# One transfer and one scaling for the queries of two neighbouring pairs, in a kernel of block-sparse attention and a gated projection

## The chip, the cores and the metric

The kernel runs on one core of one Trainium2 chip. The metric is the device time of one execution in microseconds (us), lower is better. The kernel before was timed three times: 371.8, 375.03 and 377.35 us, median 375.03 us.

## The reference

Four batches of eight heads, 768 positions in 24 blocks of 32, head size 64. A query block sees its own block, both neighbours, the first and the last block and three blocks drawn for it; the first and the last query block see all 24. The result goes through a convolution gate and two 512x512 products.

```python
scores = scale * np.matmul(q, k.transpose(0, 1, 3, 2))        # scale = 1/8
scores = np.where(mask, scores, -1000000000.0)
attn = np.exp(scores - scores.max(-1)); attn = attn / attn.sum(-1)
x = np.matmul(attn, v)                                        # [4, 768, 512]
gate = 1.0 / (1.0 + np.exp(-gate_pre))                        # gate_pre: 5 taps over xp
return (gate * (x @ w_val) @ w_out).astype(np.float32)
```

## The kernel before

**Attention.** The unit of attention work is a pair of neighbouring query blocks, all eight heads: 11 pairs in a batch and one more, called global, for the first and last block, worked off in two units. That makes 13 units in a batch and 52 in all. For a unit TensorE (PE) multiplies queries and keys (tile `sc`, for the global pair `s`), VectorE (DVE) takes the row maxima (`mx`), ScalarE (ACT) the exponentials (`pe`, `rest`, `first`), PE transposes these (`pt`), ACT or DVE copies them to SBUF (`ptr`), PE multiplies with the values (`av`), DVE divides (`rs`, `x`), PE transposes back (`xp`) and a copy puts the result in `xT`. The loop over steps n (line 764) runs three units at once: the products of unit n, the transposes of unit n-1 and the values of unit n-2.

**What a unit loads.** `load_keys` (line 323) fetches the pair's queries with one transfer into `pr.qc`, one of five buffers of 128x256 numbers (128 partitions, 1 KB each), and in passing issues the transfers of a whole batch's keys (`k`, three of 512 KB) and values (`vn`, three of 520 KB) at the places that `K_AT` and `V_AT` name. The own and the drawn key blocks are gathered in `kg`, one of four buffers: POOL (GpSimd) copies the own blocks out of `k`; of the six drawn ones POOL and ACT copy three each in batch 0, POOL copies three and SyncE (SP) fetches three from memory in batch 1, and SP fetches all six in batches 2 and 3. The values of a pair come into `va` (three buffers, by SP) and, gathered by index, into `vb` (by POOL). There is one buffer of `vn`, so the first `vn` of a batch waits until the global pair of the batch before is through with it.

**Scaling.** `scale` (line 758) multiplies the pair's queries by 1/8 in place, on ACT in batches 0 and 1 and on DVE in batches 2 and 3 (`Q_ON`), two units ahead of the products (`SCALE_AHEAD`).

**The rest.** `decode_weights` turns the 64-bit weights (`wst`, loaded at the steps of `WEIGHTS_AT`) into two float parts each (`wv`, `wo`); `gates`, `split` and `project` are the gate (`th`), the splitting of `xT` (`xh`, `xl`) and the two products (`vp`, `op`, with `y`, `yh`, `yl` between), stored through `ot`. They fill the steps: `FILLS` says how many pieces of `project` go behind each half of a unit's transposes, `STEPS` how many pieces of decoding or gate. `project` can't start before all weights are decoded.

**Order.** Each engine runs its list in the order in which the program writes it (`InOrder`, line 83), and an instruction that waits holds up all behind it on its engine. SP issues all transfers of this text but the gathers by index; `pool.tile` buffers come free when the readers of the old content are done.

Every engine operation is recorded at line 89 in the profile, so the rows are told apart by their tiles.

Of the kernel before, what the change touches and what calls it, by code (L numbers as in the profile page):

```python
# [41 lines left out]
Q_ON = "AAVV"  # L42
OWN_ON = ("VP", "DP", "AD", "PP")
LOW_ON = "PVPPPPPP"
# [3 lines left out]
GATHER = "SUGGGGGGGUGSSSSGSUGSUSSGSSGGGSSGGGGGGGGGGGSGGGGGGGGGGUGG"  # L48

SP_VALUES = ((), (), (), ())  # L50
REGS = 4

FILLS = (
    "01111112111122232210210001"
    "11000100220213041124141102"
    "12011101111120112110020111"
    "11011121112101010101210101"
    "210341"
)
STEPS = (  # L60
    "10211005213213222312211222"
    "11302202121202021241340634"
    "23200312101440051090010133"
    "22234220022240100210033013"
    "101000"
)
# [4 lines left out]
def attention_moe(ctx, tc, qb, kb, v, ve, sampled, w_val, conv_w, w_out, ident_in, slot_in, out):  # L71
# [32 lines left out]

    sb = const.tile([128, NB, NR, 2], I32, name="sb")
    src = sampled.bitcast(I32)
# [3 lines left out]
    )  # L110
    slot = const.tile([128, 2 * NB + 1], F32, name="slot")
# [4 lines left out]
    ones = two.tile([128, 128], F32, tag="y", name="ones")  # L116
    dve.memset(ones, 1.0)
    opening = ps_moe.tile([128, 512], F32, tag="mo", name="opening")
    for n in range(OPENING):
        matmul(opening[:, 0:128], ones, ones, start=n == 0, stop=n == OPENING - 1)  # L120
    warm = const.tile([128, 1], F32, name="warm")
# [3 lines left out]
    dve.tensor_copy(sm, sb[0:1, :, :, 0].rearrange("p i r -> p (i r)"))  # L125
    sf = const.tile([128, NR, NB], F32, name="sf")
    dve.tensor_copy(sf, sb[:, :, :, 0].rearrange("p i r -> p r i"))
# [9 lines left out]
    dve.memset(valid[0:32, NB - 2 : NB - 1], 0.0)  # L137
    vm = const.tile([128, NR, NB], F32, name="vm")
    tmp = const.tile([128, NR, NB], F32, name="tmp")
    dve.tensor_scalar(out=vm, in0=sf, scalar1=0.0, scalar2=None, op0=ALU.not_equal)  # L140
# [67 lines left out]
    staged = []  # L208

    def load_weights():  # L210

        for n in range(2 * CH):
            st = const.tile([128, CH, TS], F32R, tag=("xh", "xl", "yh", "yl")[n % 4], name="wst")
            flat = st.bitcast(I32).rearrange("p c n -> p (c n)")[:, 0 : 2 * DM]
            c = n % CH
            sp.dma_start(flat, (w_val if n < CH else w_out).bitcast(I32)[c * 128 : (c + 1) * 128, :])
            staged.append((step[0], flat.rearrange("p (n w) -> p n w", w=2)))
            yield
# [58 lines left out]
    def load_batch(bt):  # L277
        b = bt.b
        bt.k = two.tile([128, NB, HP * BLK], F32, tag="k", name="k")
        for h in range(3):  # L280
            sp.dma_start(bt.k[:, 8 * h : 8 * h + 8, :], kb[:, b, 8 * h : 8 * h + 8, :])
            bt.loaded += 1
            yield
        assert b == 0 or batches[b - 1].valued == 2
        bt.vn = const.tile([128, S // 128, H * DV], F32, tag="vn", name="vn")
        for c in range(3):
            r0 = b * S + 256 * c
            sp.dma_start(
                bt.vn[:, 2 * c : 2 * c + 2, :], v[r0 : r0 + 256, :].rearrange("(c p) d -> p c d", p=128)
            )  # L290
            bt.loaded += 1
            yield
# [16 lines left out]
    def block_numbers(pr, eng):  # L309
# [195 lines left out]
    def values(un):  # L505
        pr = un.pr
        if un.e == 0:
            pr.av = ps_av.tile([128, 2, 2, DV], F32, tag="av", name="av")
        if pr.glob:
# [247 lines left out]

    def scale(pr):
        if Q_ON[pr.bt.b] == "A":
            act.activation(pr.qc, pr.qc, AF.Copy, scale=0.125)  # L760
        else:
            (dve if Q_ON[pr.bt.b] == "V" else pool).tensor_scalar(out=pr.qc, in0=pr.qc, scalar1=0.125, scalar2=None, op0=ALU.mult)

    for n in range(N + LAG_X):
# [25 lines left out]
        if k < 2 * CH and n >= WEIGHTS_AT[k] and (k < 4 or k - 4 in decoded):  # L790
            next(weights)

        if n < N:
            scores(units[n])
# [7 lines left out]
        if 0 <= n - LAG_V < N:  # L802
            values(units[n - LAG_V])
            if GATHER[n] == "W":
# [3 lines left out]
        if 0 <= n - LAG_T < N:  # L808
            for half, _ in enumerate(transposes(units[n - LAG_T])):
# [70 lines left out]
```

## Time and profile before

| what | us |
|---|---|
| median of the three runs | 375.03 |
| the profiled execution | 370.94 |
| its span, first to last instruction | 369.2 |
| PE busy in the span | 341.8 (93%) |
| DVE, ACT, POOL busy | 259.5, 245.9, 216.6 |
| PE's granted clock | 0.999 of full speed |

The span is the time from the first to the last instruction of the profiled execution; 1.74 us of its 370.94 us lie around it. An engine's busy time counts its instructions alone, without issuing transfers and without waits. DMA share is the mean busy share of the core's 16 DMA engines. In a row of waits the engine named after the arrow is the one whose work came last by the profile; "issue" means that the profile shows nothing that was waited for.

### The profile page before, as it was taken

The page shows a single profiled execution, that of the slowest core. Times are in us where ns is not written, and L with a number is a line of the kernel's source. Part 1 is how long each engine was busy: PE and PEld are TensorE (multiplying, and loading weights), DVE is VectorE, ACT ScalarE, POOL GpSimd, SP SyncE. Part 2 cuts the span into 40 slices and gives each one's busy share as a digit, 9 for nine tenths or more (in the row PEclk, how much of TensorE's full clock was granted, in tenths as well). Part 3 has the DMA queues.
Part 4 walks back from the last instruction along what each step waited for, and adds up shares of the span by engine and source line. Part 5 has one row for each costly group of instructions (what it writes and reads, how often), then busy time and mean ns, then how long its engine had stood idle before and what let it go on. Part 6 is the DMA issues. An engine that isn't in the chain of part 4 may idle for free.

```text
span 369.2 us, 15557 instructions
## 1 busy us (share of the span) xinstructions
PE 341.8 (93%) x6302; PEld 275.1 (75%) x6302; DVE 259.5 (70%) x561; ACT 245.9 (67%) x594; POOL 216.6 (59%) x318
## 2 busy tenths in 40 slices
PE   8777888996899999999999999998989999999995
PEld 8455556764676977787789778886878678989893
DVE  3556847879988689975978558984958737486920
ACT  2877697898698567867685667865555768545431
POOL 1785775788896476676652665565618444525440
PEclk9999999999999999999999999999999999999999
DMA  6999986999977686797686177988644454010202
GB/s 227 317 307 283 301 268 180 267 258 313 310 200 210 182 273 178 212 314 207 185 235 203 51 201 226 270 254 225 183 151 126 124 167 143 31 60 28 85 2 86
DMA packets 52440, 72.37 MB, mean 196 GB/s; under 512 B 6928, under 2 KB 34448, under 8 KB 52368
## 3 DMA queue, kind: packets, MB, share of 16 engines
q1 hardware_dynamic: 44896, 47.82, 42.2%
q0 software_dynamic: 7040, 23.43, 22.0%
q8 instruction: 50, 0.82, 0.9%
q14 instruction: 22, 0.18, 0.2%
q10 hardware_dynamic: 432, 0.11, 0.1%
HBM read 65.05 MB, written 6.29 MB: 193 GB/s over the span
## 4 chain that ended last, share of the span: by engine, by line
PE 66%; POOL 9%; DMA 7%; ACT 5%; issue 5%; DVE 4%; SPq 2%; POOLq 1%; ACTq 0%; DVEq 0%
PE op L89 16%; PE vp L89 15%; PE av L89 12%; PE pt L89 10%; PE sc L89 8%; POOL vb L89 4%; PE xp L89 2%; DMA k<-in_k 2%; PE s L89 2%; DMA va<-in_v 2%; ACT ptr L89 2%; POOL yl L89 2%; POOL kg L89 2%; ACT pe L89 1%; SPq L89 1%
## 5 line engine op out<-in xcount | busy, mean ns | idle before, releaser
L89 POOL DMA_INDIRECT vb<-in_v,idx x88 | 89.2, 1014 | 77.3 <-PE av L89 51.2
L89 DVE SCALAR_TENSOR_TENSOR th<-xT,cw,th 128x384 f32<-128x384 f32 x128 | 92.2, 732 | 8.8 <-ACT th L89 6.6
L89 ACT ACTIVATE pe<-sc,mx 128x256 f32<-128x256 f32 x176 | 69.2, 482 | 40.6 <-DVE mx L89 40.4
L89 DVE TENSOR_REDUCE mx<-sc 128x2 f32<-128x512 f32 x88 | 56.5, 683 | 35.0 <-PE sc L89 35.0
L89 ACT COPY ptr<-pt 128x512 f32<-128x512 f32 x105 | 60.7, 610 | 8.1 <-PE pt L89 6.2
L89 POOL COPY kg<-k 128x256 f32<-128x256 f32 (+1 forms) x154 | 52.7, 381 | 9.2 <-DMA k<-in_k 9.1
L89 PE MATMUL sc<-kg,qc 64*32 64x256 f32 x1408 | 53.2, 382 | 5.2 <-issue 2.5
L89 POOL TENSOR_TENSOR yl<-y,yh 128x384 fp32r<-128x384 f32 x32 | 33.0, 1034 | 39.4 <-ACT yh L89 39.3
L89 PE MATMUL op<-wo,yh 128*128 128x512 f32 x192 | 53.7, 401 | 0.0
L89 PE MATMUL pt<-ident,pe 128*128 128x128 f32 x352 | 50.7, 280 | 2.3 <-ACT rest L89 1.4
L89 PE MATMUL vp<-xh,wv 128*128 128x384 f32 x256 | 51.5, 343 | 1.2 <-ACT ot L89 1.2
L89 PEld LDWEIGHTS av<-va,ptr 128*32 128x32 f32 (+1 forms) x1056 | 30.5, 118 | 28.6 <-issue 10.8
L89 PE MATMUL av<-va,ptr 128*32 128x65 f32 (+1 forms) x1056 | 39.6, 226 | 9.4 <-DMA va<-in_v 3.7
L89 PEld LDWEIGHTS vp<-xh,wv 128*128 128x128 f32 x256 | 43.8, 188 | 1.6 <-ACT ot L89 1.4
L89 PEld LDWEIGHTS pt<-ident,pe 128*128 128x128 f32 x352 | 38.6, 140 | 8.5 <-ACT rest L89 1.7
L89 POOL TENSOR_TENSOR xl<-xT,xh 128x384 fp32r<-128x384 f32 x32 | 33.8, 1064 | 14.2 <-ACT xh L89 14.2
L89 PEld LDWEIGHTS sc<-kg,qc 64*32 64x32 f32 x1408 | 24.6, 106 | 21.0 <-issue 6.4
L89 PEld LDWEIGHTS op<-wo,yh 128*128 128x128 f32 x192 | 35.0, 188 | 6.9
L89 PE MATMUL av<-vb,ptr 128*32 128x65 f32 x1408 | 37.9, 222 | 1.3 <-issue 1.2
L89 PE MATMUL op<-wo,yl 128*128 128x512 f32 x96 | 31.6, 410 | 1.7 <-POOL yl L89 1.7
L89 PEld LDWEIGHTS av<-vb,ptr 128*32 128x32 f32 x1408 | 29.8, 110 | 3.3 <-issue 1.5
L89 DVE SCALAR_TENSOR_TENSOR y<-th,vp 128x384 f32<-128x384 f32 x32 | 17.6, 550 | 20.9 <-PE vp L89 16.0
(74 smaller groups left out, 455.8 us busy)
## 6 DMA issues: line engine op xcount, KB each, us to landing
kg<-in_k SPq DMA_DIRECT2D x165, 64.0 KB
vn<-in_v SPq DMA_DIRECT2D x12, 520.0 KB
qc<-in_q SPq DMA_DIRECT2D x48, 128.0 KB
k<-in_k SPq DMA_DIRECT2D x12, 512.0 KB
out<-ot SPq DMA_DIRECT2D x24, 256.0 KB
va<-in_v SPq DMA_DIRECT2D x44, 130.0 KB
wst<-in_w_val SPq DMA_DIRECT2D x4, 512.0 KB
wst<-in_w_out SPq DMA_DIRECT2D x4, 512.0 KB
```

Of the source, the lines that this page charges most:

```text
L89: made = getattr(self.eng, name)(*args, **kwargs)
```

## The change

Queries are loaded and scaled for two neighbouring pairs at once. The global pair and pair 0 keep a transfer of their own; pairs 1 and 2, 3 and 4, and so on to 9 and 10 share one of 128x512 numbers (256 KB), issued where the first of the two was issued, and one operation that scales all of it, where the first of the two was scaled. There are four buffers of two pairs in place of five of one.

```diff
+    four = ctx.enter_context(tc.tile_pool(name="four", bufs=QRING))      # QRING = 4
...
+    beside = {}
+
     def load_keys(pr):
         bt, b = pr.bt, pr.bt.b
-        pr.qc = five.tile([128, HP, 2, BLK], F32, tag="qc", name="qc")
-        sp.dma_start(pr.qc, qb[:, b, pr.p + 1])
+        if pr.p <= 0 or pr.p % 2:
+            pr.group = four.tile([128, 2, HP, 2, BLK], F32, tag="qc", name="qc")
+            many = 1 if pr.p <= 0 else 2
+            (act if Q_BY[b] == "A" else sp).dma_start(pr.group[:, 0:many], qb[:, b, pr.p + 1 : pr.p + 1 + many])
+            pr.whole = pr.group[:, 0:many]
+            pr.qc = pr.group[:, 0]
+            if pr.p > 0:
+                beside[b] = pr.group
+        else:
+            pr.whole = None
+            pr.qc = beside[b][:, 1]
...
     def scale(pr):
+        if pr.whole is None:
+            return
         if Q_ON[pr.bt.b] == "A":
-            act.activation(pr.qc, pr.qc, AF.Copy, scale=0.125)
+            act.activation(pr.whole, pr.whole, AF.Copy, scale=0.125)
```

The tables of the places of loads and of the pieces of work change with it:

```diff
-V_AT = ((2, 7, 8), (0, 1, 6), (2, 2, 6), (4, 6, 7))
-K_AT = ((9, 10, 11), (7, 8, 11), (2, 10, 11), (2, 5, 8))
+V_AT = ((1, 3, 7), (0, 0, 5), (2, 2, 3), (3, 6, 7))
+K_AT = ((8, 10, 10), (7, 8, 10), (0, 8, 8), (5, 5, 11))
-WEIGHTS_AT = (1, 3, 6, 7, 8, 10, 12, 15)
+WEIGHTS_AT = (1, 3, 6, 7, 7, 10, 11, 15)
-OWN_ON = ("VP", "DP", "AD", "PP")
+OWN_ON = ("DP", "DP", "AV", "PP")
 FILLS = (
-    "01111112111122232210210001"
+    "11011111011221220322102300"
...
 STEPS = (
-    "10211005213213222312211222"
+    "10121002253203322312210222"
...
```

Smaller edits: the small tiles of the index computation (`sb`, `slot`, `sf`, `vm`, `tmp`) become parts of one of the two `th` buffers, under the name `early`; the 31 opening matmuls write the bank of `av` instead of a bank of `ps_moe`; new tables `BULK_BY` and `Q_BY` (all on SP) and `KEEP` (all zero) stand for choices that are not taken.

What moves on the engines is shown at three places. The first is SP in batch 1, where it loads the queries of the global pair and pair 4; `kg` is a fetched key block, `va` is a pair's values, `qc` queries, `vn` a third of a batch's values, and the load of a register from `sm` opens the next unit's fetch of key blocks. Before:

```order
L89 DMA kg_159<-in_k 128x128
L89 DMA va_163<-in_ve 64x520
L89 DMA va_163<-in_v 64x520
L89 DMA qc<-in_q 128x256 x2
L316 TENSOR_LOAD sm
```

and now:

```order
L94 DMA kg_158<-in_k 128x128
L94 DMA va_162<-in_ve 64x520
L94 DMA va_162<-in_v 64x520
L94 DMA qc<-in_q 128x256
L94 DMA vn<-in_v 128x2x520
L337 TENSOR_LOAD sm
```

The batch's third `vn` now stands here; before it stood one unit later, behind the next unit's three `kg` transfers, its two `va` and one more `qc`.

The second place is ACT in batch 0, the units of pairs 4 and 5; `wv` is the high part of a decoded piece of weights. Before:

```order
L89 COPY ptr<-pt 128x512 x2
L89 CAST wv_164<-words 128x512
L89 COPY xT<-xp 128x4x64
L89 ACTIVATE qc<-qc 128x256
L89 ACTIVATE pe<-sc,mx 128x256 x4
L89 COPY ptr<-pt 128x512 x2
L89 COPY xT<-xp 128x4x64
L89 ACTIVATE pe<-sc,mx 128x256 x4
L89 COPY ptr<-pt 128x512
L89 CAST wv_164<-words 128x512
L89 COPY xT<-xp 128x4x64
L89 ACTIVATE qc<-qc 128x256
```

and now:

```order
L94 COPY ptr<-pt 128x512 x2
L94 COPY xT<-xp 128x4x64
L94 ACTIVATE qc<-qc 128x256
L94 ACTIVATE pe<-sc,mx 128x256 x4
L94 COPY ptr<-pt 128x512 x2
L94 CAST wv_163<-words 128x512
L94 COPY xT<-xp 128x4x64
L94 ACTIVATE pe<-sc,mx 128x256 x4
L94 COPY ptr<-pt 128x512
L94 CAST wv_163<-words 128x512
L94 COPY xT<-xp 128x4x64
```

One cast of weights moved one unit later, and the last scaling (of pair 6, the neighbour of pair 5) is gone.

The third place is DVE in batch 3, behind the global pair. Before:

```order
L89 TENSOR_SCALAR qc<-qc 128x256
L89 TENSOR_REDUCE mx<-sc 128x2 x2
L89 SCALAR_TENSOR_TENSOR th<-xT,cw,th 128x384 x4
L89 SCALAR_TENSOR_TENSOR y<-th,vp 128x384 x2
L89 TENSOR_SCALAR qc<-qc 128x256
L89 TENSOR_REDUCE mx<-sc 128x2 x2
```

and now:

```order
L94 TENSOR_REDUCE mx<-sc 128x2 x2
L94 SCALAR_TENSOR_TENSOR th<-xT,cw,th 128x384 x4
L94 SCALAR_TENSOR_TENSOR y<-th,vp 128x384 x2
L94 TENSOR_SCALAR qc<-qc 128x512
L94 TENSOR_REDUCE mx<-sc 128x2 x2
```

The scaling of pair 6 is gone and that of pair 7 is twice as wide, at its old place. POOL's list is the same before and now, and PE's differs in the bank of the opening matmuls and at three places where transposes change places with pieces of `vp` or `op`.

## Rows read from the trace of the kernel before

**Rows 1.** Busy time by stage: us, PE, PEld, DVE, ACT, POOL, clock, DMA share, GB/s.

```profile
0.00:57.00 57.00, 46.54 (x979) 35.02 (x979) 32.74 (x99) 39.21 (x110) 36.41 (x77) 1.00 0.88 277
57.00:80.00 23.00, 20.85 (x467) 15.28 (x474) 19.20 (x46) 19.93 (x56) 15.22 (x29) 1.00 0.87 248
80.00:100.00 20.00, 14.73 (x385) 10.70 (x376) 17.42 (x36) 15.49 (x38) 18.40 (x28) 1.00 0.99 307
100.00:122.00 22.00, 20.93 (x558) 16.06 (x557) 18.46 (x39) 20.13 (x51) 16.18 (x33) 1.00 0.72 197
122.00:240.00 118.00, 118.00 (x2174) 96.91 (x2175) 90.92 (x195) 82.25 (x194) 70.99 (x87) 1.00 0.72 212
240.00:300.00 60.00, 56.30 (x1140) 45.28 (x1139) 43.83 (x88) 36.28 (x83) 32.77 (x42) 1.00 0.60 175
```

**Rows 2.** Waits of PE, 0 to 122 us: total us, times, longest.

```profile
PE av L89 <- DMA va<-in_v: 3.7, 2, 2.3
PE av L89 <- ACT ptr L89: 2.7, 5, 1.0
PE sc L89 <- issue: 2.5, 4, 1.4
...
PE pt L89 <- ACT rest L89: 1.6, 3, 1.1
...
PE av L89 <- ACT wo L89: 0.9, 1, 0.9
...
PE sc L89 <- ACT pe L89: 0.8, 1, 0.8
PE av L89 <- ACT xT L89: 0.6, 1, 0.6
```

**Rows 3.** Groups of instructions: count, busy us, mean ns, idle before.

```profile
L89 POOL COPY kg<-k 128x256 f32<-128x256 f32 x88 | 36.9, 445 | 6.9 <-DMA k<-in_k 6.8
...
L89 DVE TENSOR_SCALAR qc<-qc 128x256 f32<-128x256 f32 x24 | 13.2, 551 | 0.0
L89 ACT ACTIVATE first<-s,mx 128x512 f32<-128x512 f32 x16 | 10.9, 681 | 0.2 <-PE pt L89 0.2
L89 ACT ACTIVATE qc<-qc 128x256 f32<-128x256 f32 x24 | 10.8, 456 | 2.7 <-DMA qc<-in_q 2.7
...
L89 ACT CAST wo<-words 128x512 fp32r<-128x512 f32 x4 | 2.6, 644 | 0.2 <-DVE words L89 0.2
```

**Rows 4.** SP's transfers and a product of PE in order of time: start us, us.

```profile
56.91 0.38 SPq L89 DMA_DIRECT2D vn<-in_v  x1
...
70.99 1.09 PE L89 MATMUL sc<-kg,qc 64*32 64x256 f32 x32
...
82.03 0.42 SPq L89 DMA_DIRECT2D vn<-in_v  x1
...
85.95 0.59 SPq L89 DMA_DIRECT2D va<-in_v  x1
```

**Rows 5.** Transfers on the chain that ended last: start us, us to landing.

```profile
71.62 4.38 DMA qc<-in_q
...
91.35 7.02 DMA va<-in_v
```

**Rows 6.** The tile qc: duration ns least, median, most, first and last start.

```profile
L89 DVE TENSOR_SCALAR qc<-qc x24: 279/288/4191, 133.7 to 295.5; 128x256 f32<-128x256 f32 x24
```

**Rows 7.** Engines in order of time, 280 to 289 us.

```profile
280.61 4.19 DVE L89 TENSOR_SCALAR qc<-qc 128x256 f32<-128x256 f32 x1
...
281.03 1.00 POOL L89 TENSOR_TENSOR xl<-xT,xh 128x384 fp32r<-128x384 f32 x1
...
283.65 0.99 POOL L89 TENSOR_TENSOR yl<-y,yh 128x384 fp32r<-128x384 f32 x1
...
288.83 0.34 PE L89 MATMUL av<-va,ptr 128*32 128x65 f32 x8 [0.83 <-ACT ptr L89]
```

**Rows 8.** ACT in order of time: a scaling in batch 1.

```profile
77.58 0.46 ACT L89 ACTIVATE qc<-qc 128x256 f32<-128x256 f32 x1
```

More of the change, by code (lines that the diff above doesn't have):

```diff
@@ L48 @@
 GATHER = "SUGGGGGGGUGSSSSGSUGSUSSGSSGGGSSGGGGGGGGGGGSGGGGGGGGGGUGG"
+BULK_BY = "SSSSSSSSSSSSSSSSSSSSSSSSSSSSSSSS"
+Q_BY = "SSSS"
+KEEP = "000000000000000000000000000000000000000000000000"
 SP_VALUES = ((), (), (), ())
@@ L53 @@
 FILLS = (
-    "01111112111122232210210001"
-    "11000100220213041124141102"
-    "12011101111120112110020111"
+    "11011111011221220322102300"
+    "10012110101421303120052002"
+    "12011101111120112110021011"
     "11011121112101010101210101"
-    "210341"
+    "214301"
 )
 STEPS = (
-    "10211005213213222312211222"
[L62 to L65, printed above, removed]
+    "10121002253203322312210222"
+    "11402202121202021214340634"
+    "32120032104140051900010222"
+    "23214330202240200013023013"
+    "000111"
 )
@@ L102, in attention_moe, with part @@
     matmul, transpose = pe.matmul, pe.transpose
-    sb = const.tile([128, NB, NR, 2], I32, name="sb")
+    early = two.tile([128, CH, TS], F32, tag="th", name="early").rearrange("p c n -> p (c n)")
+    def part(first, n, *dims):
+        names = "abc"[: len(dims)]
+        sizes = dict(zip(names, dims))
+        return early[:, first : first + n].rearrange(f"p ({' '.join(names)}) -> p {' '.join(names)}", **sizes)
+    sb = part(0, 2 * NB * NR, NB, NR, 2).bitcast(I32)
     src = sampled.bitcast(I32)
@@ L110, in attention_moe @@
     )
-    slot = const.tile([128, 2 * NB + 1], F32, name="slot")
+    slot = early[:, 160 : 160 + 2 * NB + 1]
     act.dma_start(slot, slot_in)
@@ L114, in attention_moe, with turn_over @@
     act.dma_start(ident, ident_in)
-    ones = two.tile([128, 128], F32, tag="y", name="ones")
+    ones = const.tile([128, 128], F32, name="ones")
     dve.memset(ones, 1.0)
-    opening = ps_moe.tile([128, 512], F32, tag="mo", name="opening")
-    for n in range(OPENING):
-        matmul(opening[:, 0:128], ones, ones, start=n == 0, stop=n == OPENING - 1)
+    bank_of_values = [ps_av.tile([128, 512], F32, tag="av", name="av")]
+    def turn_over(times):
+        for n in range(times):
+            matmul(bank_of_values[0][:, 384:512], ones, ones, start=n == 0, stop=n == times - 1)
+    turn_over(OPENING)
     warm = const.tile([128, 1], F32, name="warm")
@@ L125, in attention_moe @@
     dve.tensor_copy(sm, sb[0:1, :, :, 0].rearrange("p i r -> p (i r)"))
-    sf = const.tile([128, NR, NB], F32, name="sf")
+    sf = part(256, NR * NB, NR, NB)
     dve.tensor_copy(sf, sb[:, :, :, 0].rearrange("p i r -> p r i"))
@@ L137, in attention_moe @@
     dve.memset(valid[0:32, NB - 2 : NB - 1], 0.0)
-    vm = const.tile([128, NR, NB], F32, name="vm")
-    tmp = const.tile([128, NR, NB], F32, name="tmp")
+    vm = part(384, NR * NB, NR, NB)
+    tmp = part(512, NR * NB, NR, NB)
     dve.tensor_scalar(out=vm, in0=sf, scalar1=0.0, scalar2=None, op0=ALU.not_equal)
@@ L208, in attention_moe, with queue @@
     staged = []
+    def queue(n):
+        return act if BULK_BY[n] == "A" else sp
     def load_weights():
@@ L215, in load_weights @@
             c = n % CH
-            sp.dma_start(flat, (w_val if n < CH else w_out).bitcast(I32)[c * 128 : (c + 1) * 128, :])
+            queue(24 + n).dma_start(flat, (w_val if n < CH else w_out).bitcast(I32)[c * 128 : (c + 1) * 128, :])
             staged.append((step[0], flat.rearrange("p (n w) -> p n w", w=2)))
@@ L280, in load_batch @@
         for h in range(3):
-            sp.dma_start(bt.k[:, 8 * h : 8 * h + 8, :], kb[:, b, 8 * h : 8 * h + 8, :])
+            queue(3 * b + h).dma_start(bt.k[:, 8 * h : 8 * h + 8, :], kb[:, b, 8 * h : 8 * h + 8, :])
             bt.loaded += 1
@@ L287, in load_batch @@
             r0 = b * S + 256 * c
-            sp.dma_start(
+            queue(12 + 3 * b + c).dma_start(
                 bt.vn[:, 2 * c : 2 * c + 2, :], v[r0 : r0 + 256, :].rearrange("(c p) d -> p c d", p=128)
@@ L507, in values @@
         if un.e == 0:
-            pr.av = ps_av.tile([128, 2, 2, DV], F32, tag="av", name="av")
+            bank_of_values[0] = ps_av.tile([128, 512], F32, tag="av", name="av")
+            pr.av = bank_of_values[0][:, 0 : 4 * DV].rearrange("p (a h d) -> p a h d", a=2, h=2)
         if pr.glob:
@@ L758, in scale @@
     def scale(pr):
+        if pr.whole is None:
+            return
         if Q_ON[pr.bt.b] == "A":
-            act.activation(pr.qc, pr.qc, AF.Copy, scale=0.125)
+            act.activation(pr.whole, pr.whole, AF.Copy, scale=0.125)
         else:
-            (dve if Q_ON[pr.bt.b] == "V" else pool).tensor_scalar(out=pr.qc, in0=pr.qc, scalar1=0.125, scalar2=None, op0=ALU.mult)
+            (dve if Q_ON[pr.bt.b] == "V" else pool).tensor_scalar(
+                out=pr.whole, in0=pr.whole, scalar1=0.125, scalar2=None, op0=ALU.mult
+            )
     for n in range(N + LAG_X):
@@ L791, in attention_moe, with keep @@
             next(weights)
+        def keep(place):
+            turn_over(int((KEEP + "0000")[min(4 * n, len(KEEP)) + place]))
         if n < N:
+            keep(0)
             scores(units[n])
@@ L802, in attention_moe @@
         if 0 <= n - LAG_V < N:
+            keep(1)
             values(units[n - LAG_V])
@@ L808, in attention_moe @@
         if 0 <= n - LAG_T < N:
-            for half, _ in enumerate(transposes(units[n - LAG_T])):
+            turned = transposes(units[n - LAG_T])
+            for half in range(len(units[n - LAG_T].P)):
+                keep(2 + min(half, 1))
+                next(turned)
                 at_half = 2 * n + min(half, 1)
```

1 line of the change is left out of this document (added).

## Prediction

> **What bounds the kernel now.** I read the stage table first [rows 1], because the share of the whole span says little here: PE is busy 93%, yet the idle rest isn't spread evenly. From 122 to 240 us PE has no idle time at all. Its idle time is 10.46 us before 57 us (57.00 - 46.54), 2.15 us from 57 to 80, 5.27 us from 80 to 100, 1.07 us from 100 to 122, and 3.70 us from 240 to 300. So the change can gain in two places only: in batches 0 and 1, which have no projection to fill with, at most 18.95 us, part of it the start; and between 240 and 300 us, at most 3.70 us. In the saturated stretch a saving on another engine is hidden by PE's own work, and PE's work is the same before and after.
>
> The waits of PE before 122 us say what ended these gaps [rows 2]. Two waits for the transfer of `va` make 3.7 us. Those that end on ACT (`ptr`, `rest`, `wo`, `pe`, `xT`) make 2.7 + 1.6 + 0.9 + 0.8 + 0.6 = 6.6 us, and the products `sc` that wait for something that isn't named 2.5 us; these stand where ACT is late with freeing a score bank, so I count 9.1 us to ACT. In the same stages the DMA engines are 0.88, 0.87 and 0.99 busy [rows 1]. ACT and the transfers are what the change touches.
>
> **Part A: scaling on ACT, batches 0 and 1.** Removed are 24 operations of 128x256 at a mean of 456 ns, 10.9 us [rows 3]. Added are 4 of 128x256 (global pair and pair 0, twice), 1.8 us, and 10 of 128x512. The trace has no such scaling of 128x512, but casts of that size on ACT from SBUF to SBUF at 644 ns and exponentials from PSUM at 681 ns [rows 3]; the cast is nearer in source and destination: 6.4 us. Bounds: twice the narrow one, 912 ns, and the narrow one itself, 456 ns. So ACT has 10.9 - 8.2 = 2.7 us less to do. Not all of it reaches PE: a saving counts only in units in which PE waits for ACT. The five rows of ACT waits together with the unnamed ones have 15 waits in 26 units [rows 2], but some units have two; I take half of the units, 1.3 us. The other end is a loss: a wide scaling stands 0.19 us longer (644 - 456) before its unit's exponentials than the narrow one, and if just the ten units with a wide one are those on the path, PE loses 1.9 us. Range of the part: 1.9 us lost to 2.7 gained; taken: 1.3 gained.
>
> **Part B: the transfers.** 48 transfers become 28, 20 of them of 256 KB; the bytes stay the same. SP takes 0.38 to 0.59 us to issue a transfer [rows 4], so it issues some 20 x 0.45 = 9 us less over the kernel, half of that in batches 0 and 1. Where SP waits, this saves nothing: at 56.91 us it gets past the first `vn` of batch 1, which has to wait for the buffer [rows 4], and `V_AT` leaves that `vn` at the same place; all transfers ahead of it are the same ones in both kernels. Behind it order matters, for PE's two waits for `va` are due to transfers issued around 85.95 and 91.35 us [rows 4, 5], the second of which took 7.02 us to land while the DMA engines were 0.99 busy. The third `vn` stood just ahead, at 82.03 us, and now goes out one unit earlier, into a stage with 0.13 of 23 us free [rows 1], 3.0 us. Its 520 KB take 1.7 us at the stage's 307 GB/s; against that, the second half of a wide query transfer comes a unit earlier, 128 KB, 0.43 us. Taken: 1.7 - 0.4 = 1.3 us of the 3.7. Bounds: all 3.7 us gained; or nothing gained and 0.4 lost, if the free share doesn't lie where the `vn` now falls. The second `vn` now goes ahead of the first three `kg` of batch 1, which it delays by its 1.7 us; the products that need them start at 70.99 us [rows 4], 14 us behind that `vn`, which hides it.
>
> The Trainium skill (DMA: Bandwidth & Descriptors, section Bandwidth, Measured) says to batch transfers to 1 MiB or more for three quarters of the peak rate; its section on the anatomy of one DMA fits about 2 us of fixed cost to each, there for transfers that GpSimd issues. By that, as an estimate, 20 fewer transfers would be worth 40 us if they ran one behind the other. In the stage that matters the engines are 0.99 busy with several transfers at a time, so the fixed part lies beside other transfers; the sum goes without it, and the mechanism has its rival below.
>
> **Part C: scaling on DVE, batches 2 and 3.** Again 24 become 14, 10 of them wide. DVE spends 13.2 us on the 24, 551 ns each [rows 3], but the median is 288 ns and one took 4191 ns [rows 6]. That one stands beside a row of POOL instructions without a gap, from 281.03 to 284.64 us, and ends 0.16 us after them [rows 7]: DVE was held up, the maxima behind it were late, and PE waited 0.83 us for `ptr` soon after [rows 7]. Nothing says that this place is mended: POOL's list is unchanged, and the scaling that stood there stands there still, twice as wide. All others lie where PE is saturated or has no such wait. Taken: 0; bounds 1.2 us either way, the 0.83 and the like wait before it.
>
> The Trainium skill (SBUF — State Buffer, section Who interferes with whom) says that a DVE `tensor_scalar` can run in a mode in which it and a GpSimd instruction exclude each other, whoever comes first holding the port for the whole instruction. The row agrees in kind, but 4.19 us is the length of several POOL instructions, not of one. By the rule fewer scalings mean fewer such meetings, and the sum would gain up to the 1.2 us; by the row the meeting at 280.61 us stays.
>
> **Part D: the rest.** `OWN_ON[b]` in `copy_keys` reads the `b` of the function around it, which is 3 once the loops over batches are through; so all pairs use "PP" before and after, which the 88 copies of 128x256 on POOL (two for each of 44 pairs) confirm [rows 3]. The edit does nothing. Nor do `BULK_BY`, `Q_BY` and `KEEP`. `early` holds a `th` buffer that isn't needed until batch 0 is nearly through; the opening matmuls run on PE ahead of any `av`, so that bank costs no wait. `FILLS` moves three pieces on PE by a few matmuls, 0. `STEPS`, `WEIGHTS_AT` and `K_AT` move decoding by a unit and keys to earlier places; I see no wait that one of them ends or makes, and take 0. For their bounds I take one late cast of weights per batch, 0.9 us as in [rows 2], twice: 1.8 us either way.
>
> **Sum.** 1.3 + 1.3 + 0 + 0 = 2.6 us. The profiled execution, 370.94 us, would come to 368.3 us. It lies 4.1 us under the median of its own kernel; for a median I keep that distance: 375.03 - 2.6 = 372.4 us.
>
> **Rivals.**
> Nothing gained (375.0 us). ACT's saving falls into its own idle time and the `vn` only exchanges one wait for another. For it: ACT works 94.8 of the first 122 us (the sum of its busy time over four stages of [rows 1]), so it has 27 us of slack somewhere. Against: PE's waits for it are spread over many units.
>
> The cost per transfer is what holds batches 0 and 1 (366.5 us). Then fewer transfers free SP and the queue, and the whole of A and B comes: 2.7 + 3.7 us, with C's 1.2 and half of D's bound, 0.9: 8.5 us, that is 366.5. For it: the queries issued at 71.62 us took 4.38 us to land [rows 5], ten times what their bytes take at 307 GB/s. Against: 0.99 DMA share at 307 GB/s speaks for bytes, and those don't change. The rule on batching of the Trainium skill (DMA: Bandwidth & Descriptors, section Bandwidth) would show itself here in this way.
>
> The pair's transfer comes late (379.5 us, slower). A pair's queries are scaled on ACT one unit after their transfer is issued, and ACT runs in order. The transfer issued at 71.62 us landed after 4.38 us, at 76.0 [rows 5]; ACT scaled at 77.58 [rows 8], 5.96 us after the issue. A wide one lands 0.43 us later, still in time; but one that takes as long as the `va`, 7.02 + 0.43 us, makes ACT stand for 1.5 us, with the exponentials of a unit behind it. Three wide transfers of batch 1 fall into the busy stages: 4.5 us, 379.5 us; if all ten of batches 0 and 1 come late, 390. It decides from 5.96 us of landing on. Against: before, ACT waited for queries 2.7 us in all, at the start alone [rows 3].
>
> **How the numbers follow.** Forecast 0.52, nothing gained 0.21, cost per transfer 0.17, late transfer 0.10. A measurement of this kernel can tell about 2%, 7.5 us: faster is below 367.5, slower above 382.5. Most of the third case (0.13) and a tail of the forecast (0.02) lie below, 0.15; the worse part of the last (0.06) and 0.01 of table moves above, 0.07; 0.78 remain. The forecast's own range is 369.5 to 375. The range given runs from the third case, less the rest of D's bound (365.6), to the late transfer at three pairs (379.5).
>
> **What would show it.** Right: 14 scalings on ACT of 8 to 8.5 us in all; PE's waits for `va` before 100 us down from 3.7 to about 2.4; PE without idle time from 122 us, shifted earlier by some 2.5 us; DVE's long scaling near 280 us still there. Wrong: waits of ACT for `qc` after the start (late transfer); a DMA share in the first 57 us well under 0.88 with PE's waits gone (cost per transfer); PE's idle time before 122 us still near 19 us (nothing gained). If DVE's long scaling is gone and the time from 240 us on is shorter, part C was read wrongly; if a late piece of weights puts the first `vp` off, part D was.

## The result and the profile after

The changed kernel takes 375.42 us (median of 22 runs, 371.45 to 382.05), the kernel before 372.88 us (22 runs, 369.75 to 378.47): a ratio of 1.0062, 95% interval 1.0034 to 1.0089, so 0.6% slower where 0.7% faster was forecast. The ratios here and below leave disturbed runs out. The profiled execution of the changed kernel took 377.68 us and lies above its median, the one of before (370.94) below its own; the two profiles are 6.7 us apart, the medians 2.5. What follows shows where one long execution of the changed kernel loses time against one short execution of the kernel before; what it is worth, the experiments say.

The stage table of the changed kernel, with the columns of [rows 1]:

```profile
0.00:57.00 57.00, 47.18 (x979) 35.94 (x979) 33.59 (x102) 40.17 (x109) 35.54 (x76) 0.97 0.85 277
57.00:80.00 23.00, 21.86 (x502) 16.45 (x503) 20.53 (x46) 20.38 (x55) 18.62 (x32) 1.00 0.95 285
80.00:100.00 20.00, 14.99 (x339) 10.76 (x338) 14.31 (x27) 12.45 (x29) 17.53 (x27) 0.91 0.97 288
100.00:122.00 22.00, 18.57 (x430) 13.86 (x430) 16.06 (x35) 16.07 (x38) 12.84 (x23) 0.84 0.48 139
122.00:240.00 118.00, 114.93 (x2136) 94.13 (x2132) 87.33 (x186) 81.36 (x191) 70.93 (x93) 1.00 0.69 202
240.00:300.00 60.00, 57.44 (x1098) 46.73 (x1104) 47.06 (x87) 39.04 (x89) 34.06 (x43) 1.00 0.64 187
```

PE's waits up to 122 us, as in [rows 2]:

```profile
PE av L94 <- DMA vb<-in_v,idx: 4.8, 3, 2.3
PE pt L94 <- ACT rest L94: 3.9, 3, 2.0
PE sc L94 <- DVE th L94: 2.1, 1, 2.1
PE av L94 <- ACT ptr L94: 1.7, 4, 1.0
PE av L94 <- ACT qc L94: 1.5, 1, 1.5
...
PE s L94 <- DVE rs L94: 1.2, 1, 1.2
```

The waits for `va`, 3.7 us in [rows 2], are gone. In their place stand waits for the gathers `vb` (4.8), for `rest` (3.9 instead of 1.6) and for DVE (2.1 + 1.2). And the granted clock, 1.00 in every row of [rows 1], is 0.84 from 100 to 122 us. How much each counts in these two profiles is read at one point that both kernels pass with the same products behind them, the first `vp`. PE's row from the start to it, before and after:

```profile
0.00:121.72 121.72, 102.76 (x2374) 1.00 0.87 262
```

```profile
0.00:127.44 127.44, 108.04 (x2378) 0.95 0.81 249
```

The first `vp` comes 5.72 us later. PE's idle time up to it is 127.44 - 108.04 = 19.40 us, before 121.72 - 102.76 = 18.96: 0.44 us more. Its busy time for the same products is 5.28 us longer, and the clock is 0.95 in place of 1.00. So nearly all of the difference between these two profiles up to here stands in PE's busy time, not in its waits. The rest, 1.0 us, comes later: from 122 to 240 us PE is idle for 3.07 us where it had no idle time, and gets 1.14 us back from 240 to 300 and 0.87 behind that.

Two things limit this reading, as the same row shows of two kernels that lose nothing, e11 and e8 (the experiments describe them):

```profile
0.00:122.95 122.95, 106.31 (x2375) 0.99 0.84 259
```

```profile
0.00:125.46 125.46, 110.16 (x2374) 0.99 0.84 254
```

First, busy time is more than the clock. At 0.99 it is 3.55 and 7.40 us above that of the kernel before; time between the products of one group counts as busy too (the 192 products `s` up to 122 us are 6.7 us busy before and 10.2 in e8, at 381 and 382 ns each). Second, one profile isn't the kernel: the first `vp` comes at 125.46 us in e8, in a set where the kernel before was slower too, but also at 126.51 in e1, the same kernel in a set where it was not. So the 5.72 us are not the loss of the change.

Where the clock falls is seen on PE in order of time (changed kernel, waits in brackets):

```profile
37.36 0.30 PE L94 MATMUL av<-vb,ptr 128*32 128x65 f32 x2
39.98 0.72 PE L94 MATMUL av<-vb,ptr 128*32 128x65 f32 x30 [2.32 <-DMA vb<-in_v,idx]
40.63 1.97 PE L94 MATMUL pt<-ident,pe 128*128 128x128 f32 x8
...
76.19 1.09 PE L94 MATMUL pt<-ident,pe 128*128 128x128 f32 x8
...
82.02 1.09 PE L94 MATMUL av<-vb,ptr 128*32 128x65 f32 x30 [1.51 <-DMA vb<-in_v,idx]
83.04 1.94 PE L94 MATMUL pt<-ident,pe 128*128 128x128 f32 x8
...
89.86 2.25 PE L94 MATMUL s<-k,qc 64*32 64x256 f32 x48 [1.15 <-DVE rs L94]
...
94.92 1.09 PE L94 MATMUL pt<-ident,pe 128*128 128x128 f32 x8 [1.60 <-ACT rest L94]
...
101.37 1.52 PE L94 MATMUL pt<-ident,first 128*128 128x128 f32 x8 [2.01 <-ACT rest L94]
...
115.30 2.04 PE L94 MATMUL sc<-kg,qc 64*32 64x256 f32 x30 [2.05 <-DVE th L94]
...
120.44 1.09 PE L94 MATMUL sc<-kg,qc 64*32 64x256 f32 x32
```

Eight transposes take 1.09 us at 76.19 and 1.97 at 40.63, right behind a wait of 2.32 us; the scores, 1.09 us at 120.44, take 2.04 behind a wait of 2.05. PE's windows around these places (PE busy, granted clock, DMA share, GB/s) give a clock of 0.66, 0.53 and 0.57, a mix of stretches at 2.4 and at 1.2 GHz:

```profile
40.00:45.00 5.00, 5.00 (x94) 0.66 0.98 294
...
82.00:85.00 3.00, 2.98 (x40) 0.53 1.04 274
...
115.00:119.00 4.00, 3.70 (x74) 0.57 0.08 22
```

Not every such wait has this behind it: at 94.92 us the transposes run at full speed behind 1.60 us, and before, a wait of 2.29 us for `va` (the longest in [rows 2]) left the clock at 1.00 from 80 to 100 us [rows 1].

The two long waits for `vb` end with these gathers (start, us to landing):

```profile
31.95 7.99 DMA vb<-in_v,idx
...
74.40 7.58 DMA vb<-in_v,idx
```

SP issued bulk loads just ahead of them:

```profile
30.99 1.25 SPq L94 DMA_DIRECT2D k<-in_k  x2
...
73.78 0.43 SPq L94 DMA_DIRECT2D vn<-in_v  x1
```

That these loads made the gathers late is not shown. Over all 88 gathers the times to landing (least, median, most) are nearly the same in the kernel before and in the changed one:

```profile
DMA to landing us min/median/max: 3.5/5.0/7.9
```

```profile
DMA to landing us min/median/max: 3.4/5.3/8.1
```

PE also comes to the first of the two gathers earlier, at 37.66 us, and starts most of the products on it at 39.98, where the kernel before starts them at 39.16 without a wait.

The `vn` of 73.78 us is the third one of batch 1, which stood at 82.03 us [rows 4] and whose earlier place part B counted as a gain. At 77.43 us the changed kernel begins the scores that the kernel before begins at 79.69, 2.3 us earlier; at the global pair of batch 1 it is behind (89.86 against 88.46).

Last, the order on DVE and ACT at this place, which no row ahead of the prediction shows. Before, ACT makes the first `th` of a tile at 80.36 us, and DVE takes it up without a wait:

```profile
80.36 0.65 ACT L89 ACTIVATE th<-xT,cw 128x384 f32<-128x384 f32 x1
```

```profile
84.95 0.60 DVE L89 SCALAR_TENSOR_TENSOR th<-xT,cw,th 128x384 f32<-128x384 f32 x1
```

After, ACT makes it at 86.14, two pieces together and behind two copies of `ptr`. DVE, which runs in order, stands 2.19 us for it, with the maxima of the next unit behind; the next two pieces take 2.98 us, beside a row of `xl` on POOL, and the `s` products of 89.86 us and the transposes of 94.92 and 101.37 wait for what is late by that:

```profile
86.14 1.13 ACT L94 ACTIVATE th<-xT,cw 128x384 f32<-128x384 f32 x2
```

```profile
86.79 1.53 DVE L94 SCALAR_TENSOR_TENSOR th<-xT,cw,th 128x384 f32<-128x384 f32 x1 [2.19 <-ACT th L94]
88.25 1.28 DVE L94 TENSOR_REDUCE mx<-sc 128x2 f32<-128x512 f32 x2
...
90.19 2.98 DVE L94 SCALAR_TENSOR_TENSOR th<-xT,cw,th 128x384 f32<-128x384 f32 x2
```

The code shows where the order comes from. `prepare` first asks the decoding of weights for a piece, and only where that has none does it advance the gates. Weights that arrive a unit earlier, or steps that are dealt out otherwise, give decoding a piece more at this place, and the gate starts later, in the same step as its first piece on DVE.

The scalings themselves came out as worked out in part A:

```profile
L94 ACT ACTIVATE qc<-qc 128x512 f32<-128x512 f32 x10 | 6.7, 666 | 0.0
L94 ACT ACTIVATE qc<-qc 128x256 f32<-128x256 f32 x4 | 1.8, 440 | 2.4 <-DMA qc<-in_q 2.4
```

### The profile page after: what moved, and what is told of

The parts are those of the page before. It is cut to its first block, busy times and chain, and to the rows that moved or that the text cites. A ratio compares the mean times of both kernels' runs of the same rounds, so it can differ in the third digit from the quotient of the medians.

```text
span 375.9 us, 15511 instructions
## 1 busy us (share of the span) xinstructions
PE 347.0 (92%) x6302; PEld 279.5 (74%) x6302; DVE 259.6 (69%) x551; ACT 246.1 (65%) x584; POOL 219.2 (58%) x318
## 4 chain that ended last, share of the span: by engine, by line
PE 59%; DVE 12%; DMA 9%; POOL 7%; issue 5%; ACT 3%; SPq 3%; POOLq 1%; ACTq 0%; DVEq 0%
PE vp L94 16%; PE op L94 13%; PE av L94 10%; PE pt L94 9%; PE sc L94 7%; DVE th L94 5%; DMA vb<-in_v,idx 4%; POOL vb L94 3%; DVE mx L94 3%; POOL kg L94 3%; SPq L94 2%; PE xp L94 2%; DMA k<-in_k 2%; DMA kg<-in_k 2%; DVE qc L94 1%
## 5 line engine op out<-in xcount | busy, mean ns | idle before, releaser
L94 POOL DMA_INDIRECT vb<-in_v,idx x88 | 87.6, 995 | 80.1 <-PE av L94 60.1
L94 DVE SCALAR_TENSOR_TENSOR th<-xT,cw,th 128x384 f32<-128x384 f32 x128 | 96.2, 763 | 12.3 <-ACT th L94 10.0
L94 POOL COPY kg<-k 128x256 f32<-128x256 f32 (+1 forms) x154 | 56.5, 405 | 8.7 <-DMA k<-in_k 8.5
L94 PE MATMUL sc<-kg,qc 64*32 64x256 f32 x1408 | 54.0, 390 | 3.5 <-DVE th L94 2.1
L94 PE MATMUL pt<-ident,pe 128*128 128x128 f32 x352 | 52.4, 286 | 3.0 <-ACT rest L94 1.6
L94 PEld LDWEIGHTS pt<-ident,pe 128*128 128x128 f32 x352 | 40.1, 144 | 9.4 <-issue 2.3
```

Source lines behind the costliest of these rows:

```text
L94: made = getattr(self.eng, name)(*args, **kwargs)
```

## The experiments

Beside each set the kernel before ran on the same chip. Its median was 373.1 to 373.6 us beside all runs but the second set (e5 to e8), where it was 378.08; so only ratios are compared. Three theories at the start: places (earlier bulk loads delay gathers), steps (pieces of decoding and gating stand ahead of the maxima), merge (the wide transfer or scaling costs more than it saves).

**First set: the merging and the tables apart.** e1 is the changed kernel with all five tables of before:

```
-V_AT = ((1, 3, 7), (0, 0, 5), (2, 2, 3), (3, 6, 7))
-K_AT = ((8, 10, 10), (7, 8, 10), (0, 8, 8), (5, 5, 11))
-WEIGHTS_AT = (1, 3, 6, 7, 7, 10, 11, 15)
+V_AT = ((2, 7, 8), (0, 1, 6), (2, 2, 6), (4, 6, 7))
+K_AT = ((9, 10, 11), (7, 8, 11), (2, 10, 11), (2, 5, 8))
+WEIGHTS_AT = (1, 3, 6, 7, 8, 10, 12, 15)
...
```

with `FILLS` and `STEPS` likewise. e2 is the kernel before with the five new tables, e3 the changed kernel with these three lines alone put back, e4 with `FILLS` and `STEPS` alone put back.

> The changed kernel with all five tables of the kernel before (V_AT, K_AT, WEIGHTS_AT, FILLS, STEPS): the merged transfers and scalings and the small edits alone. Places theory (the earlier bulk loads delay gathers of vb, and PE idles and then runs at the lower clock): the waits of PE for vb, 4.8 us in the profile of the changed kernel, are gone, and the time is that of the kernel before or 1 to 2.6 us less (370 to 373 where the kernel before has 373). Steps theory (pieces of decoding and gating stand ahead of the maxima on DVE): the same time, for the tables are the old ones here too; the waits for DVE th and ACT rest of 2 us each are gone. Merge theory (the wide transfer or the wide scaling costs more than it saves): still 2 to 3 us slower than the kernel before.

> The kernel before with the five tables of the changed kernel; its queries come and are scaled pair by pair as before. Places theory and steps theory: 2 to 4 us slower than the kernel before, with waits of PE for vb near 40 and 82 us (places) or for DVE th near 115 us (steps). Merge theory: the time of the kernel before, within 0.3%.

> The changed kernel with V_AT, K_AT and WEIGHTS_AT of the kernel before; FILLS and STEPS stay new. Places theory: the two waits for vb (2.3 at 40 us, 1.5 at 82 us) go, the granted clock between 80 and 100 us is back at 1.0, and the time falls by 3 to 5 us to that of the kernel before or below it. Steps theory: no gain over the changed kernel; the waits for DVE th and ACT rest stay. Merge theory: no gain either, and waits that end on qc stay.

> The changed kernel with FILLS and STEPS of the kernel before; the loads stay at their new places. Steps theory: the 2 us waits for ACT rest near 101 us and for DVE th near 115 us go, the clock from 100 to 122 us is back at 1.0, and the time falls by 3 to 5 us. Places theory: the waits for vb near 40 and 82 us stay, and the time gains 1 us at most. Merge theory: no gain.

Measured: e1 0.9971 (0.9932 to 1.0010), e2 1.0200 (1.0147 to 1.0253, 6 runs), e3 1.0038 (0.9994 to 1.0083), e4 1.0067 (1.0026 to 1.0107). The merge theory falls: merged transfers alone don't cost, and tables alone cost most. Where the steps are put back (e4) a loss stays; where the places are put back (e3) the middle value stays 0.7% above e1, though the interval doesn't tell it from the kernel before. So the places can't be left out of the cause, and the steps perhaps can't either. Both theories had expected more: e3 still waits 2.9 us for `vb` in all, and e4, with old steps, keeps the waits for `rest` and DVE; its clock from 100 to 122 us is 0.84.

**Second set: which part of the merging gains.** e5 is e1 with queries loaded and scaled pair by pair as before, the small edits alone. e6 splits the scaling, e7 the transfer:

```
-            pr.whole = pr.group[:, 0:many]
-            pr.qc = pr.group[:, 0]
+            pr.qc = pr.whole = pr.group[:, 0]
...
-            pr.whole = None
-            pr.qc = beside[b][:, 1]
+            pr.qc = pr.whole = beside[b][:, 1]
```

```
-            (act if Q_BY[b] == "A" else sp).dma_start(pr.group[:, 0:many], qb[:, b, pr.p + 1 : pr.p + 1 + many])
+            for j in range(many):
+                sp.dma_start(pr.group[:, j], qb[:, b, pr.p + 1 + j])
```

e8 is e1 once more.

> The kernel before with the small edits alone: the early buffer, the tile of ones, the opening products in the bank of av, the empty tables. Queries come and are scaled pair by pair, and the five tables are the old ones. If the merging is what made the first experiment 0.3% faster than the kernel before, the time here is that of the kernel before, within 0.3%. If the small edits did it (the opening products no longer hold a bank that the first products want), it is 1 to 2 us under the kernel before, as the first experiment was, and the merging is worth nothing with the old tables.

> The first experiment with two narrow scalings for each wide transfer, 24 on ACT and 24 on DVE as in the kernel before. If the wide scaling is worth what the prediction gave it, 1.3 us, the time lies that much above the first experiment, half way to the kernel before; ACT then has 24 scalings of some 456 ns, 10.9 us in all against some 8.2. If the transfers made the gain, the time is that of the first experiment, within 0.3%.

> The first experiment with two narrow transfers for each wide one, both issued where the wide one is, and the wide scaling kept: 48 transfers of queries instead of 28. If a transfer has a cost of its own in the first 122 us (the rival of the prediction), the time is 2 us or more above the first experiment. If the bytes alone count, it is the same within 0.3%.

> The first experiment once more, on the same chip as its two parts: 0.3% under the kernel before, or, if that was the scatter of the runs, the time of the kernel before. In the profile PE has no wait of half a microsecond between 126 and 240 us, as before.

Measured: e5 1.0018 (0.9987 to 1.0048), e6 0.9969 (0.9940 to 0.9997), e7 1.0015 (0.9981 to 1.0048), e8 0.9952 (0.9923 to 0.9980). The small edits do nothing. The gain of the merging is there again, 0.5% here, and splitting the transfers takes it back: 1.0015 - 0.9952 = 0.63%, 2.4 us of 378 (0.7 to 4.0 by the two intervals), for 20 transfers more. Splitting the scaling takes back 0.17%, 0.6 us, which the intervals don't tell from nothing. Where the 2.4 us lie, the profiles of e7 and e8 (spans 376.3 and 375.9 us) don't show.

**Third set: which rows of the tables.** The tables have a row for each batch (`FILLS` and `STEPS` a last one for the tail). e9 has new rows for batches 0 and 1 and the new `WEIGHTS_AT`, e10 new rows for batches 2 and 3; both are merged. e11 is e1 with one number changed:

```
-V_AT = ((2, 7, 8), (0, 1, 6), (2, 2, 6), (4, 6, 7))
+V_AT = ((2, 7, 8), (0, 1, 5), (2, 2, 6), (4, 6, 7))
```

and e12 is the changed kernel itself.

> The changed kernel with the tables' new rows for batches 0 and 1 (and the new WEIGHTS_AT), and the old rows for batches 2 and 3. If the loss comes from the first 122 us (gathers behind earlier bulk loads, DVE late, the lower clock behind the gaps), the time stays that of the changed kernel, 0.6% above the kernel before. If it comes from the waits that the changed kernel has between 150 and 191 us (DVE ptr 0.78, DVE mx 1.52, ACT xT 0.77, 3.1 us together), these go, and the time is that of the kernel before or below it.

> The other half: old rows for batches 0 and 1 (and the old WEIGHTS_AT), new rows for batches 2 and 3. If the loss comes from the waits between 150 and 191 us, they are here, 3.1 us, and the time is 2 to 3 us above that of the merging with all tables old (which was 0.3 to 0.5% under the kernel before). If it comes from the first 122 us, the time is that of the merging with all tables old.

> The merging with all tables old, but for the one place on which part B of the prediction rests: the third vn of batch 1 goes out one unit earlier (V_AT of batch 1 is 0, 1, 5). The prediction's step: the waits of PE for va near 92 and 100 us shrink and the time falls by 1.3 us. Rival: DVE is as late there as the transfer, so waits that end on DVE or on ACT's exponentials behind it (DVE rs, ACT rest) take the place of the waits for va, and the time stays within 0.3%.

> The changed kernel itself on the chip of its parts: 0.3 to 0.9% above the kernel before, with the waits of PE for DVE ptr, DVE mx and ACT xT between 150 and 191 us as in its first profile.

Measured: e9 1.0052 (1.0010 to 1.0094), e10 0.9961 (0.9928 to 0.9995), e11 0.9963 (0.9913 to 1.0012), e12 1.0100 (1.0039 to 1.0161). The loss sits in the rows of batches 0 and 1: 1.0052 - 0.9961 = 0.91%, 3.4 us (1.4 to 5.4 by the two intervals), the same as from e1 to the changed kernel (1.0062 - 0.9971). The rows of batches 2 and 3 cost nothing; e10 is as quick as e1. Of the waits that the changed kernel has between 150 and 191 us (0.78, 1.52 and 0.77 us) the profile of e9 has one of 0.79 and that of e10 one of 0.77, so they don't mark the half that costs. In the profile of e11 PE's waits for `va` of 0.7 us and more (1.53 and 2.53 in e1) are gone, as part B said, and two for `rest` stand there, as its rival said:

```profile
95.41 1.09 PE L94 MATMUL pt<-ident,pe 128*128 128x128 f32 x8 [1.23 <-ACT rest L94]
...
100.75 1.09 PE L94 MATMUL pt<-ident,first 128*128 128x128 f32 x8 [0.90 <-ACT rest L94]
```

Its time can't be told from that of e1. Nor is it shown that the third `vn` did this: in the profiles of e8, which is the kernel of e1, and of e17 below, both with this `vn` at its old place, PE has no listed wait for `va` up to 122 us either.

**Fourth set: the clock, and places or steps.** e13 is the changed kernel with products that nothing uses, where PE waits (for each unit four digits: how many ahead of the scores, the values and the two transposes), e14 the same for e1 at its own waits:

```
-KEEP = "000000000000000000000000000000000000000000000000"
+KEEP = "0000000000000000000000000500000000000000000000000000000000000300000000400050000000005000"
```

e15 is e1 with the new places of batches 0 and 1 alone, e16 with the new steps of these batches alone.

> The changed kernel with 22 products more that compute nothing that is used (128x128, some 0.31 us each in the opening, 6.9 us in all), placed where its PE waits: 5 ahead of the value products that wait for vb at 40 us, 3 at 82 us, 4 and 5 ahead of the transposes that wait for ACT rest at 95 and 101 us, 5 ahead of the scores that wait for DVE th at 115 us. If the lower clock behind these waits is the price, the granted clock in the first 122 us rises (0.84 from 100 to 122 us before), and the time falls by 1 to 3 us from that of the changed kernel, to within 0.3% of the kernel before, although PE has more to do. If the clock is only a companion, the time stays at 0.6 to 1.0% above the kernel before, or rises by as much of the 6.9 us as the waits don't hide.

> The merging with all tables old and 13 such products: 2 and 4 and 5 ahead of the value products at 21, 94 and 101 us, 2 ahead of the scores at 115 us. If the clock is the price: 0.2 to 0.5% under the merging alone, that is 0.6 to 0.9% under the kernel before. If it isn't: the time of the merging alone or 1 us more.

> The merging with the new places of loads (V_AT, K_AT of the first two rows, WEIGHTS_AT) and old steps. If the places cost: 0.4 to 0.7% above the kernel before, that is some 0.9% above the merging alone, with waits of PE for vb or for ACT's casts of weights in the first 60 us. If the steps cost: the time of the merging alone, 0.3 to 0.5% under the kernel before.

> The merging with the new FILLS and STEPS of batches 0 and 1 and the old places of loads. If the steps cost: 0.4% or more above the kernel before, with waits of PE that end on DVE or on ACT rest between 85 and 122 us. If the places cost: the time of the merging alone, 0.3 to 0.5% under the kernel before.

Measured: e13 1.0046 (1.0008 to 1.0083), e14 1.0033 (0.9998 to 1.0067), e15 1.0081 (1.0051 to 1.0111), e16 1.0004 (0.9974 to 1.0035). e15 and e16 against e1 (0.9971, 0.9952): the new places of batches 0 and 1 cost 1.1 to 1.3%, the new steps 0.3 to 0.5%, the latter hardly told from nothing by the intervals. e13 and e14 don't settle the clock. e13 is no slower than the changed kernel although PE has 22 products more, and the clock from 100 to 122 us is 0.93 in its profile; but its products had a price of their own, for those in the bank of `av` stood behind the reading of that bank:

```profile
PE av L94 <- DVE x L94: 4.4, 2, 2.9
```

e14, with 13 of them, lies 0.6% above e1.

**Fifth set: one load.** The profiles of the changed kernel, of e9 and of e15 all have a wait of 2.1 to 2.8 us for `vb` near 41 us, beside two loads of keys in one unit. e17 is e1 with that edit alone, e18 is e15 with it undone:

```
-K_AT = ((9, 10, 11), (7, 8, 11), (2, 10, 11), (2, 5, 8))
+K_AT = ((8, 10, 10), (7, 8, 11), (2, 10, 11), (2, 5, 8))
```

> The merging with old tables, but K_AT of batch 0 is 8, 10, 10 instead of 9, 10, 11: two loads of keys go out in one unit. If they are what delays the gather, PE waits 2 us for vb near 41 us, and the time lies 0.4 to 1.0% above the merging alone. If the cost is spread over the other places (vn, weights, batch 1), the time is that of the merging alone within 0.3%.

> The new places of loads with the merging and old steps (0.8% above the kernel before), but K_AT of batch 0 old. If the two loads of keys are the cause, the wait for vb near 41 us is gone and the time is 0.4 to 1.0% lower, at or under that of the kernel before. If not, it stays 0.6 to 0.9% above it.

Measured: e17 0.9869 (0.9816 to 0.9923), e18 1.0076 (1.0039 to 1.0113). The idea is refuted both ways. Alone, the edit makes the kernel quicker; undone, it gives nothing back, although the wait near 41 us is gone in e18. And e17 has the two loads in one unit without that wait: its longest for `vb` is 0.8 us. e17, 369.43 us (365.48 to 373.37, 6 runs) beside 373.55, is quicker than both kernels. PE's row to its first `vp`, the time of the kernel before with 1.2 us less idle time (121.62 - 103.86 = 17.76 us) and the clock at 1.00:

```profile
0.00:121.62 121.62, 103.86 (x2375) 1.00 0.86 263
```

**What the slower kernels have in common.** In every kernel with the new rows for batches 0 and 1, of places or of steps, DVE's first `th` behind 80 us waits 2.1 to 2.2 us for ACT; in no other does it wait, e11 and e17 with one new number each among them. e16 has it with old places, e18 with old steps:

```profile
88.39 1.54 DVE L94 SCALAR_TENSOR_TENSOR th<-xT,cw,th 128x384 f32<-128x384 f32 x1 [2.19 <-ACT th L94]
```

```profile
86.81 1.63 DVE L94 SCALAR_TENSOR_TENSOR th<-xT,cw,th 128x384 f32<-128x384 f32 x1 [2.10 <-ACT th L94]
```

and e17 is without it:

```profile
84.22 0.62 DVE L94 SCALAR_TENSOR_TENSOR th<-xT,cw,th 128x384 f32<-128x384 f32 x1
```

Ordered by it (clock: mean granted clock of PE over the runs of that kernel; the kernel before had 0.990 to 0.992):

| wide transfers | first `th` on DVE | kernels: ratio | clock |
|---|---|---|---|
| no | no wait | before 1; e5 1.0018; e7 1.0015 | 0.990 to 0.992 |
| yes | no wait | e1 0.9971; e6 0.9969; e8 0.9952; e10 0.9961; e11 0.9963; e17 0.9869 | 0.990 to 0.995 |
| yes | waits 2.1 to 2.2 us | changed 1.0062, again 1.0100; e3 1.0038; e4 1.0067; e9 1.0052; e15 1.0081; e16 1.0004; e18 1.0076 | 0.975 to 0.989 |
| no | waits 2.1 us | e2 1.0200 | 0.983 |

Among the kernels with wide transfers the two groups don't overlap, in time or in clock, though their nearest members do by their intervals (e1 0.9932 to 1.0010, e16 0.9974 to 1.0035). e13 and e14, with products added, are left out. In e15 and e18 it can only be `WEIGHTS_AT` that moved the `th`, since the other two tables place loads on SP alone (the lists of DVE and ACT are the same in e1, e11 and e17). In e15 and e18 ACT's list differs from that of e1 at this place alone: the first `th` and a cast of `wo` have changed places, so that the `th` comes a unit later; on DVE three pieces of decoding come a unit earlier. So the rivals left for the cost of the places are this order and the loads themselves. No run moved the `th` by itself, so that it is the cause, and not something that came with it, is argued and not shown. Against its being all of the cause speaks that the wait is the same in e16 (2.19 us) and e15 (2.10), while their losses against e1 are 0.3% and 1.1%.

## Why the prediction was wrong

The sum was 2.6 us gained; measured are 2.5 us lost between the medians. The merging by itself gained 0.3% (e1) to 0.5% (e8), 1.1 to 1.8 us, and the tables took it back and more: 3.4 us against e1, 4.1 against e8.

**Part D is the step that failed**: "I see no wait that one of them ends or makes, and take 0", with bounds of 1.8 us either way. The new tables of batches 0 and 1 cost 3.4 us by their middle value (e9 against e10, and the changed kernel against e1), nearly twice the bound. They hold the `V_AT` of part B as well, whose third `vn` in batch 1 costs nothing measurable by itself (e11). The bound was made from a late cast of weights on ACT, and the term overlooked waits that the new order does make. In the profile of the changed kernel PE waits 3.9 us for `rest` instead of 1.6 and 3.3 us for DVE; a piece more of decoding puts the start of the gate into the same step as its first piece on DVE, which then stands 2.2 us with the maxima of a unit behind it. All kernels with the new rows have this wait on DVE, so asking of each piece that moved what it waits for on its engine would have shown it. How much of the 3.4 us it makes stays open. The other halves of part D held: `OWN_ON` and the small edits, 0 (e5), the tables of batches 2 and 3, 0 (e10).

**Part B** gave no gain that a run shows. The waits for `va` are gone in the changed kernel, all 3.7 us where 1.3 were taken, but the profiles of e8 and e17 have none either with the third `vn` at its old place, so that this `vn` made them isn't borne out. Nor was its new place worth anything: e11 has waits for `rest` instead and no time of its own. "The sum goes without it", said of the cost of a transfer, was wrong: 20 transfers fewer are worth 2.4 us (e7 against e8), 0.12 us each. So the rival of the cost per transfer was right in kind, with 2.4 us in place of its 8.5. The Trainium skill (DMA: Bandwidth & Descriptors, section Bandwidth, Measured) had the sign, by its rule to batch transfers; the 40 us estimated from the fixed cost on that page are 17 times what the runs show.

**Part A**: ACT spends 6.7 + 1.8 = 8.5 us on 14 scalings, where 8.2 were worked out and 8 to 8.5 given as the sign; wide ones take 666 ns (644 taken), narrow ones 440. On the path 1.3 us were taken; e6 against e8 gives 0.6, not told from 0. The loss of its lower bound is not seen: PE's one longer wait for ACT's `qc`, 1.5 us at 29.12 us, stands behind a narrow scaling of 0.43 us, and the second profile of the same kernel (e12) is without it.

**Part C** held. The long scaling is still there, with a row of POOL instructions beside it, and PE waits 0.45 us for `ptr` soon after, where it waited 0.83 [rows 7]:

```profile
288.44 4.32 DVE L94 TENSOR_SCALAR qc<-qc 128x512 f32<-128x512 f32 x1
```

```profile
288.86 1.01 POOL L94 TENSOR_TENSOR xl<-xT,xh 128x384 fp32r<-128x384 f32 x1
...
291.48 0.99 POOL L94 TENSOR_TENSOR yl<-y,yh 128x384 fp32r<-128x384 f32 x1
```

**What bounds the kernel** was read too narrowly. PE's idle time was taken for all that could change before 122 us. Between the two profiles it hardly changed (18.96 and 19.40 us to the first `vp`); the busy time for the same products did, with the granted clock. The profile shown had the clock at 1.00 in every row, 0.999 over its span, against a mean of 0.990 to 0.992 over all runs of that kernel: a favourable execution taken for the usual one. That the clock is the price is suggested by profiles (e9: 17.13 us idle, less than before, and the first `vp` 4.5 us later at a clock of 0.92) and by the runs: the mean clock of the changed kernel is 0.984, and within the kernel before 0.01 less clock goes with 1.3 to 3.2 us more time (a fit to the runs beside each set). But a clock that falls behind waits is their companion too, and e13 did not settle which it is.

The late transfer of the third rival did not come: ACT waits for queries at the start alone (2.4 us), DVE once for 0.4. "Nothing gained" came nearest in the time (375.0), but by luck: its 375.03 was the median of three runs, 2.15 us above that of 22, and two effects of opposite sign stand behind the result, not none.

Open stay what in the new order costs the time, the wait on DVE or another; which of `V_AT`, `WEIGHTS_AT` and `K_AT` carries the cost of the places; why e17 (6 runs) gains 0.8 to 1.0% over e1; and where in the profile the gain of the wide transfers lies.

## What to carry to other kernels

Split such a change into its mechanical part and its tables before judging it: here the first gained 0.3 to 0.5%, and the tables hid it. Where instructions of several jobs share an engine that runs in order, an input that comes earlier isn't safe: it can shift a job behind the engine that feeds it, as the `th` here. And before explaining a difference by two profiles, look at a second profile of the same kernel: here the point taken for the loss, the first `vp`, comes as late in a kernel that loses nothing.

## What the hardware showed that was not expected

- The granted clock behind waits of PE: in the changed kernel eight transposes took 1.97 us behind a wait of 2.32 us, 1.09 us elsewhere. The length of one wait doesn't decide it: a wait of 2.29 us for `va` was followed by transposes of 1.09 us in the kernel before, and the same wait at the same place by transposes of 1.97 us in e10:

```profile
93.85 1.09 PE L89 MATMUL pt<-ident,pe 128*128 128x128 f32 x8 [0.30 <-ACT rest L89]
```

```profile
92.78 0.69 PE L94 MATMUL av<-va,ptr 128*64 128x65 f32 x16 [2.29 <-DMA va<-in_v]
...
94.15 1.97 PE L94 MATMUL pt<-ident,pe 128*128 128x128 f32 x8
```

- 20 transfers fewer, 28 instead of 48 at the same bytes, were worth 2.4 us (e7 against e8; 0.7 to 4.0 by the intervals).
- The kernel before took 373.1 to 373.6 us beside four of the sets and 378.08 beside the second, while its mean granted clock was 0.990 to 0.992 beside all of them. The record gives the second set the same chip number as the first, so what slowed it stays open; the ratios of e1 and e8, the same kernel in each, agree within their intervals.
